# The first layer's w_in in four tiles of four slices, folded with 512 moving columns

## The chip, the cores and the metric

One core of a Trainium2 chip runs the kernel. The metric is the device time of one execution in microseconds (us), the median over several runs. Engines are called as the profile calls them: PE (TensorE matmul), PEld (its weight load), DVE (VectorE), ACT (ScalarE), POOL (GpSimd), SP (SyncE, which issues nearly all DMAs).

## The reference

An attention between tokens and a small state, then two layers of the form "matmul, nonlinearity, matmul" on the 2304 rows that it returns. Shapes: B=4, H=8, S=512 tokens and Ns=32 states per batch, D=64; model width 512, hidden width 2048. All is float32; the weights arrive as float64.

```python
scores = scale * np.matmul(x, state.transpose(0, 1, 3, 2))
a = np.exp(scores - scores.max(-1, keepdims=True))
a /= a.sum(-1, keepdims=True) + 1e-09
xread = np.matmul(a, state)                      # 512 rows per batch
...                                              # sread: the same with x and state exchanged, 32 rows per batch
x = rows of concatenate([xread, sread], axis=2)  # (2304, 512)
h = x @ w_in;  g = np.where(h > 0, h, np.exp(np.minimum(h, 0)) - 1);            x = g @ w_out
h = x @ w_in2; g = h * np.tanh(np.log1p(np.exp(np.minimum(h, 20)))); out = g @ w_out2
```

## The kernel before

**Folding.** For the tokens of batch b, xread is a product of the softmax `a` with the state, so `xread @ w_in` equals `a @ (state @ w_in)`. The kernel makes the small product m = state @ w_in once per batch (`fold`, the matmul at L523) and multiplies the softmax by it (L755, or L769 to L771), so the full w_in of the first layer is used only by the folds and by the 128 rows of the states (L745). A fold multiplies one head's 32 states by 64 rows of w_in: eight matmuls, two on the array's rows by four on its columns, lie side by side in the array, each with its own weights of 64 x 32. One call `fold(b, j0, j1)` makes m for the slices j0 to j1 of w_in (a slice is 128 of the 2048 hidden columns): it takes two PSUM banks, issues eight matmuls per step of at most two slices (so 256 moving columns), and then copies both banks to `m` (L532). A float32 matmul has two records in the trace: where the program's order says x2, the trace says x4.

**Tiles.** w_in of the first layer lies in eight tiles `w1[j // 2]` of two slices each, under the tag "w_in" of 16 buffers of 4 KB per partition. The 16 products m (four per batch, four slices each) and the 16 slices of the second layer's w_in use the same tag.

**Staging of weights.** `weight` loads a slice of float64 (L430 for the first w_in, two DMAs of 256 KB; L436 for w_out), ACT makes `wy` of its high words (L446), DVE adds the low bits and the sign (L455, L457, L468 into the w1 tile, L474 or L478 for w_out). The second layer's weights go through DRAM and come back by `reload` and `split_weight`.

**Steps.** A step is one slice j of one batch: `mm1` (h = softmax x m), `hidden` (ACT exp L788, ACT L791, DVE L795 or L798) and, two steps later, `mm2` (four accumulations acc, one per 128 tokens). The first eight steps (batch 0, slices 0 to 7) run in whole float32: h by L755, and acc by L837 for the first six of them. Later steps split each operand in two float32r parts, three matmuls each (L769 to L771, L849 to L851). Then come batch 1 with slices 0 to 7, batches 0 and 1 with slices 8 to 15, batches 2 and 3, and the second layer. Before batch b can run, `token_reads(b, hf)` makes its softmax: it loads x (`xb`, L556, two DMAs of 256 KB for each of two halves hf), transposes it on PE (`xT`, L600: two groups of four transposes, one for each DMA), makes scores (L638), the softmax on DVE and ACT, and transposes that (`pT`, L663).

**What sets the order.** No order is written by hand. `Plan.run` simulates the engines with the costs given to `add` and places next, engine by engine, the operation that can start first (ties go to the earlier due time). An operation can start when its predecessors have ended and its buffers are free; the DMA queues have a rate, `RATE` = 330 bytes per ns, and a latency of 2 us in that simulation. The result is a fixed instruction order on each engine, and an engine waits at an instruction whose semaphore has not come, whatever stands behind it. A fold's cost is given as

```python
step = min(2, j1 - j0)
...
for j in range(j0, j1, step):
    A("PE", 0.1 + mm(4 * step * P), lambda j=j: f(j), w=[(pt, j) for pt in pts], place=[m, *pts],
      lag=FOLD_AHEAD if (b, j0) == (STATES_AFTER[0], STATES_AFTER[1] + 1) else FOLD_LAG,
      r=[("sd", b, 0), ("sd", b, 1)] + [(w1[i // 2], i % 2) for i in range(j, j + step)])
```

Batch 0 makes its first eight slices by `FIRST_FOLDS` in five calls of 1, 1, 2, 2 and 2 slices, as the weights arrive; every other m is one call of four slices, in two steps of two.

Of the kernel before, what the change touches and what calls it, by code (L numbers as in the profile page):

```python
# [40 lines left out]
class Buf:  # L41
# [6 lines left out]

    def __getitem__(self, i):
        return self.t[i]  # L50


class Op:
# [162 lines left out]
def attention_elu_mish(  # L216
# [190 lines left out]
    w1, w_sb, w_back = {}, {}, {}  # L407

    def place_w1(j, k):
        return w1[j // 2].t.rearrange("p (k f) -> p k f", k=NK)[:, k, j % 2 * P:(j % 2 + 1) * P]  # L410

    loads = itertools.count()

    def weight(kind, layer, j, due=None):
        i = next(loads)
        soon = i < EARLY
        due = -20.0 + i if i < RAW_FIRST else due
        name = f"{kind}{layer}_{j}_"
# [25 lines left out]


        add("ACT", 0.68, lambda: nc.scalar.activation(y.t, words()[0].bitcast(F32), AF.Copy, scale=2.0 ** -112),  # L446
            r=[raw], w=[y])
        signs = layer == 1 and Z_FROM <= j < Z_TO
        if signs:

            add("ACT", 0.68, lambda: nc.scalar.activation(v.t, y.t, AF.Identity, bias=negative, scale=2.0 ** -60),
                r=[y, "negative"], w=[v])
        else:

            add("DVE", 0.43, lambda: nc.vector.tensor_scalar(u32(v), u32(y), 3, None, ALU.logical_shift_left),  # L455
                r=[y], w=[v])
        add("DVE", 0.69, lambda: nc.vector.scalar_tensor_tensor(  # L457
            u32(v), words()[1], 29, u32(v), ALU.logical_shift_right, ALU.bitwise_or), r=[raw, v], w=[v])
        last = (3, ALU.logical_shift_left) if signs else (0x80000000, ALU.bitwise_and)
        if kind == "in" and layer == 1:  # L460
            if j // 2 not in w1:
                w1[j // 2] = buf("w", "w_in", NF, [P, NK * 2 * P], F32, f"w1_{j // 2}_")
            to = w1[j // 2]

            def sign():
                o = to.t.bitcast(U32).rearrange("p (k f) -> p k f", k=NK)[:, :, j % 2 * P:(j % 2 + 1) * P]
                a, c = (u32(i).rearrange("p (k f) -> p k f", k=NK) for i in (y, v))
                nc.vector.scalar_tensor_tensor(o, a, last[0], c, last[1], ALU.bitwise_or)  # L468

            add("DVE", 0.69, sign, r=[y, v], w=[(to, j % 2)])  # L470
            return
        if layer == 1 and j < WHOLE_OUT:
            w = w_sb["whole", layer, j] = buf("w", f"w_{kind}", NF, [P, DM], F32, f"whole{j}_")
            add("DVE", 0.69, lambda: nc.vector.scalar_tensor_tensor(  # L474
                u32(w), u32(y), last[0], u32(v), last[1], ALU.bitwise_or), r=[y, v], w=[w])
            after_step.setdefault(index[1, 0, j], []).append(j)
            return
        add("DVE", 0.69, lambda: nc.vector.scalar_tensor_tensor(  # L478
            u32(v), u32(y), last[0], u32(v), last[1], ALU.bitwise_or), r=[y, v], w=[v])
        if layer == 2:  # L480
            add(SP, 256.0, lambda: nc.sync.dma_start(out=w2d[:, kind == "out", j, :], in_=v.t),
                r=[v], w=[("w2d", kind, j)])
            return
        split_weight(kind, layer, j, v)

    after_step = {}

    def split_weight(kind, layer, j, v):
        w = w_sb[kind, layer, j] = buf("w", f"w_{kind}", NF, [P, 2, DM], F32R, f"w_{kind}{layer}_{j}_")
        add(EITHER, {"ACT": 0.61, "DVE": 0.43}, lambda e: copy(e, w[:, 0, :], v.t), r=[v], w=[(w, 0)])  # L490
        lo, cost = (nc.gpsimd, {"POOL": 1.3}) if (kind, layer, j) in POOL_LO else (nc.vector, {"DVE": 0.69})
        add(next(iter(cost)), cost, lambda: lo.tensor_tensor(
            w[:, 1, :], v.t, w[:, 0, :].bitcast(F32), ALU.subtract), r=[v, (w, 0)], w=[(w, 1)])

    def reload(kind, j):
        v = buf("work", "wraw", 3, [P, DM], F32, f"back_{kind}_{j}_")
# [6 lines left out]

    def m_tile(b, c):
        if (b, c) not in m_sb:
            m_sb[b, c] = buf("w", "w_in", NF, [P, 2, DM], F32, f"m{b}_{c}_")
        return m_sb[b, c]

    def fold(b, j0, j1):
# [2 lines left out]
        m = m_tile(b, j0 // NC)  # L512
        pts = [bank("fold") for e in range(2)]
        n = (j1 - j0) * P
        step = min(2, j1 - j0)

        def f(j):
            w = w1[j // 2].t.rearrange("p (k f) -> p k f", k=NK)
            c = slice(j % 2 * P, (j % 2 + step) * P)
            for k in range(NK):  # L520
                for e in range(2):
                    r, l = slice(e * D, (e + 1) * D), slice(k * NS, (k + 1) * NS)
                    nc.tensor.matmul(pts[e][l, (j - j0) * P:(j - j0 + step) * P], lhsT=sd[b][r, e, k, e, :],  # L523
                                     rhs=w[r, k, c], start=True, stop=True, tile_position=(e * D, k * NS))

        for j in range(j0, j1, step):
            A("PE", 0.1 + mm(4 * step * P), lambda j=j: f(j), w=[(pt, j) for pt in pts], place=[m, *pts],
              lag=FOLD_AHEAD if (b, j0) == (STATES_AFTER[0], STATES_AFTER[1] + 1) else FOLD_LAG,
              r=[("sd", b, 0), ("sd", b, 1)] + [(w1[i // 2], i % 2) for i in range(j, j + step)])
        cols = slice(j0 % NC * P, j0 % NC * P + n)  # L530
        for e in range(2):
            A(EITHER, both(n), lambda g, e=e: copy(g, m[:, e, cols], pts[e][:, :n]),  # L532
# [203 lines left out]
    def mm1(s):  # L736
# [4 lines left out]
        if kind == 0:  # L741
            for i in range(NC):
                def f(i=i):
# [3 lines left out]

                sl = j * NC + i
                A("PE", 4 * mm(4 * P), f, w=[h], due=due,
                  r=[(w1[sl // 2], sl % 2)] + [("sread", b) for b in range(B)])  # L750
        elif kind == 1 and (blk, j) in WHOLE:
            for k in range(2):
                def f(k=k):
# [5 lines left out]
        else:  # L759
            nk = 2 if kind == 1 else NK  # L760
            for k in range(nk):
# [12 lines left out]
                    r = [(m_hl[s], 0), (m_hl[s], 1), (x1hl(blk), k)]  # L774
                else:
                    w = w_sb["in", 2, j]
                    r = [(w, 0), (w, 1), (x2[blk][0], k), (x2[blk][1], k)]
                add("PE", 3 * mm(n), f, r=r, w=[h], due=due)
        return h

# [282 lines left out]
```

## Time and profile before

| | us |
|---|---|
| device time, median of 3 runs (lowest, highest) | 753.88 (753.29, 753.99) |
| span of the profiled execution | 751.1 |
| PE busy in 0 to 20 of the span | 11.91 |
| PE busy in 20 to 45 | 23.30 |
| PE busy in 45 to 60 | 14.65 |
| PE busy in 60 to 80 | 20.00 |
| PE busy in 80 to 100 | 18.57 |
| PE busy in 100 to 742 | 641.69 |
| DVE busy in 20 to 45, and in 60 to 80 | 23.18, 18.70 |

Between 100 and 742 us PE is busy without a break, so there only its own work counts; what it waits for is found in the first 100 us. A timeline row gives the start, the length, the engine, the line, the tiles (out<-in), the shape, the count, and in brackets the idle time ahead of it with what ended it. A matmul's length contains the pipeline behind it; the time that it takes from its neighbours is the distance from its start to the next start.

### The profile page before, as it was taken

To read this page: it belongs to the slowest core of one execution; us is meant where nothing else is said; L and a number is where in the kernel's file an instruction comes from. 1 tells how busy PE (TensorE), PEld (TensorE's weight loads), DVE (VectorE), ACT (ScalarE), POOL (GpSimd) and SP (SyncE) were. 2 spreads that over 40 slices of the span, in tenths; PEclk is the share of its full clock that TensorE was granted. 3 is DMA by queue.
4 is the path that set the end of the run, shared out by engine and by line. 5 is a ranking of instruction groups with operands and counts; after the bars stand their busy time and mean duration, and the time that the engine had idled before them with its cause. 6 is when DMAs were issued, how large, how long until landed. Compare 5 with 4: busy or idle time off the path is not lost.

```text
span 751.1 us, 11051 instructions
## 1 busy us (share of the span) xinstructions
PE 732.6 (98%) x4098; PEld 598.0 (80%) x4098; DVE 556.8 (74%) x1048; ACT 425.0 (57%) x759; POOL 10.6 (1%) x27
## 2 busy tenths in 40 slices
PE   5899999999999999999999999999999999999996
PEld 5346677788777879878888888888889999999995
DVE  6988899988689895798999856565567565756564
ACT  3674767655567663577657445454455455545443
POOL 1000000010000000000000000000000000000000
PEclk8899999999999999999999999999999999999999
DMA  9953667453585543665845103000030020001001
GB/s 227 291 154 101 166 161 215 117 169 113 147 256 175 189 140 104 189 196 185 283 162 193 42 1 99 0 1 1 0 99 1 1 83 2 1 1 42 1 1 42
DMA packets 67292, 81.71 MB, mean 109 GB/s; under 512 B 22696, under 2 KB 45992, under 8 KB 67240
## 3 DMA queue, kind: packets, MB, share of 16 engines
q1 hardware_dynamic: 65028, 80.36, 36.1%
q10 hardware_dynamic: 2212, 0.66, 0.4%
q8 instruction: 32, 0.52, 0.3%
q14 instruction: 20, 0.16, 0.1%
HBM read 59.51 MB, written 21.50 MB: 108 GB/s over the span
## 4 chain that ended last, share of the span: by engine, by line
PE 94%; DMA 2%; DVE 1%; ACT 1%; issue 0%; SPq 0%; ACTq 0%
PE acc_acc L849 16%; PE acc_acc L851 15%; PE acc_acc L850 15%; PE h L769 12%; PE h L771 12%; PE h L770 12%; PE fold L523 2%; PE acc_acc L837 2%; PE h L745 2%; PE h L755 2%; DMA raw_in<-in_moe_w_in 2%; PE scores L638 1%; PE pT L663 1%; PE sr L697 1%; DMA xb<-in_x 1%; PE xT L600 1%
## 5 line engine op out<-in xcount | busy, mean ns | idle before, releaser
L788 ACT ACTIVATE e<-h 128x512 f32<-128x512 f32 (+1 forms) x148 | 83.2, 562 | 118.2 <-PE h L771 106.5
L813 ACT CAST g<-e 128x512 fp32r<-128x512 f32 (+1 forms) x142 | 82.4, 581 | 61.9 <-PE acc_acc L851 25.6
L771 PE MATMUL h<-x,w_in 128*128 128x384 f32 (+1 forms) x320 | 114.6, 358 | 0.0
L769 PE MATMUL h<-x,w_in 128*128 128x384 f32 (+1 forms) x320 | 114.4, 358 | 0.0
L770 PE MATMUL h<-x,w_in 128*128 128x384 f32 (+1 forms) x320 | 114.3, 357 | 0.0
L814 DVE TENSOR_TENSOR g<-e,g 128x512 fp32r<-128x512 f32 (+1 forms) x142 | 91.1, 642 | 22.5 <-ACT g L813 21.7
L851 PE MATMUL acc_acc<-w_out,g 128*128 128x512 f32 x272 | 106.9, 393 | 0.0
L850 PE MATMUL acc_acc<-w_out,g 128*128 128x512 f32 x272 | 106.7, 392 | 0.0
L849 PE MATMUL acc_acc<-w_out,g 128*128 128x512 f32 x272 | 105.9, 389 | 0.4 <-ACT g L813 0.4
L849 PE MATMUL acc_acc<-g,w_out 128*128 128x512 f32 x232 | 93.3, 402 | 0.0
L810 DVE TENSOR_TENSOR u<-u,e 128x384 f32<-128x384 f32 (+1 forms) x80 | 48.9, 611 | 57.7 <-ACT e L809 57.6
L850 PE MATMUL acc_acc<-g,w_out 128*128 128x512 f32 x232 | 90.5, 390 | 0.0
L851 PE MATMUL acc_acc<-g,w_out 128*128 128x512 f32 x232 | 90.5, 390 | 0.0
L808 ACT ACTIVATE e<-u,two 128x384 f32<-128x384 f32 (+1 forms) x80 | 52.8, 660 | 50.1 <-DVE u L806 49.9
L805 DVE TENSOR_SCALAR e<-e 128x384 f32<-128x384 f32 (+1 forms) x80 | 30.9, 387 | 48.2 <-ACT e L788 48.1
L769 PEld LDWEIGHTS h<-x,w_in 128*128 128x128 f32 x320 | 60.1, 188 | 7.1
L770 PEld LDWEIGHTS h<-x,w_in 128*128 128x128 f32 x320 | 60.1, 188 | 7.1
L771 PEld LDWEIGHTS h<-x,w_in 128*128 128x128 f32 x320 | 60.1, 188 | 5.0
L851 PEld LDWEIGHTS acc_acc<-w_out,g 128*128 128x128 f32 x272 | 51.0, 187 | 11.0 <-DVE g L814 0.3
L849 PEld LDWEIGHTS acc_acc<-w_out,g 128*128 128x128 f32 x272 | 51.1, 188 | 10.1 <-ACT g L813 0.9
L850 PEld LDWEIGHTS acc_acc<-w_out,g 128*128 128x128 f32 x272 | 51.0, 188 | 9.5
L849 PEld LDWEIGHTS acc_acc<-g,w_out 128*128 128x128 f32 x232 | 43.5, 188 | 13.5 <-issue 3.3
(126 smaller groups left out, 1169.7 us busy)
## 6 DMA issues: line engine op xcount, KB each, us to landing
raw_out<-in_moe_w_out SPq DMA_DIRECT2D x32, 512.0 KB, 4.3
raw_in<-in_moe_w_in SPq DMA_DIRECT2D x32, 256.0 KB, 7.3
raw_in<-in_moe_w_in SPq DMA_DIRECT2D x16, 512.0 KB, 4.2
w2d<-wv SPq DMA_DIRECT2D x32, 256.0 KB, 3.4
xb<-in_x SPq DMA_DIRECT2D x16, 256.0 KB, 4.2
x2d<-o SPq DMA_DIRECT2D x16, 256.0 KB, 2.6
xb<-in_x SPq DMA_DIRECT2D x32, 128.0 KB, 3.9
back_in<-w2d SPq DMA_DIRECT2D x16, 256.0 KB, 3.0
```

Source lines behind the costliest of these rows:

```text
L769: nc.tensor.matmul(h[:, :n], lhsT=wh, rhs=xh, start=(k == 0), stop=False)
L770: nc.tensor.matmul(h[:, :n], lhsT=wh, rhs=xl, start=False, stop=False)
L771: nc.tensor.matmul(h[:, :n], lhsT=wl, rhs=xh, start=False, stop=(k == nk - 1))
L788: add("ACT", act(n), lambda: nc.scalar.activation(E(), Hh(), AF.Exp), r=[h], w=[e])
L805: add("DVE", 0.1 + 0.00065 * n, lambda: nc.vector.tensor_scalar(E(), E(), E20, None, ALU.min), r=[e], w=[e])
L808: add("ACT", act(n) + 0.12, lambda: nc.scalar.activation(E(), U(), AF.Ln, bias=two), r=[u, "two"], w=[e])
L810: add("DVE", dve(n), lambda: nc.vector.tensor_tensor(U(), U(), E(), ALU.mult), r=[u, e], w=[u])
L813: add("ACT", act(n) + 0.01, lambda: nc.scalar.copy(g[:, 0, :n], E()), r=[e], w=[(g, 0)])
L814: add("DVE", dve(n), lambda: nc.vector.tensor_tensor(g[:, 1, :n], E(), g[:, 0, :n].bitcast(F32), ALU.subtract), r=[e, (g, 0)], w=[(g, 1)])
L849: nc.tensor.matmul(acc.t, lhsT=st[:, 0, :], rhs=mv[:, 0, :], start=fst, stop=False)
L850: nc.tensor.matmul(acc.t, lhsT=st[:, 0, :], rhs=mv[:, 1, :], start=False, stop=False)
L851: nc.tensor.matmul(acc.t, lhsT=st[:, 1, :], rhs=mv[:, 0, :], start=False, stop=lst)
```

## The change

The eight w1 tiles become four of four slices each (8 KB per partition), under a new tag "w_wide" of four buffers; the tag "w_in" shrinks from 16 to 8 buffers. A fold takes all its slices in one step: 512 moving columns where it makes four slices, one group of eight matmuls where there were two of 256 columns. Batch 0's first five calls keep their 1, 1, 2, 2 and 2 slices. In the second layer, slices 4 to 11 of w_in lie two to a tile in the "w_wide" buffers (`Half`), and the other eight in "w_in". The lines below L48 of the changed kernel stand 14 to 22 lines lower than before.

```diff
+class Half:
+    def __init__(self, base, i):
+        self.base, self.i = base, i
+    def __getitem__(self, i):
+        return self.base.t[:, self.i][i]
+
+def part(w, i):
+    return (w.base, w.i, i) if isinstance(w, Half) else (w, i)
...
-        return w1[j // 2].t.rearrange("p (k f) -> p k f", k=NK)[:, k, j % 2 * P:(j % 2 + 1) * P]
+        return w1[j // NC][:, k, j % NC * P:(j % NC + 1) * P]
...
-                w1[j // 2] = buf("w", "w_in", NF, [P, NK * 2 * P], F32, f"w1_{j // 2}_")
+                w1[j // NC] = buf("w", "w_wide", NF // NC, [P, NK, NC * P], F32, f"w1_{j // NC}_")
...
+        if kind == "in" and NC <= j < NF - NC:
+            if j % 2 == 0:
+                pairs[j // 2] = buf("w", "w_wide", NF // NC, [P, 2, 2, DM], F32R, f"w_pair{j // 2}_")
+            w = Half(pairs[j // 2], j % 2)
+        elif kind == "in":
+            w = buf("w", "w_in", NF // 2, [P, 2, DM], F32R, f"w_{kind}{layer}_{j}_")
...
-            m_sb[b, c] = buf("w", "w_in", NF, [P, 2, DM], F32, f"m{b}_{c}_")
+            m_sb[b, c] = buf("w", "w_in", NF // 2, [P, 2, DM], F32, f"m{b}_{c}_")
...
-        step = min(2, j1 - j0)
+        step = j1 - j0
...
-            c = slice(j % 2 * P, (j % 2 + step) * P)
+            c = slice(j % NC * P, (j % NC + step) * P)
...
-              r=[("sd", b, 0), ("sd", b, 1)] + [(w1[i // 2], i % 2) for i in range(j, j + step)])
+              r=[("sd", b, 0), ("sd", b, 1)] + [(w1[i // NC], i % NC) for i in range(j, j + step)])
```

The planner then places other work. PE before, early in the program, from the first h of batch 0 on (`sd_79` is the state of batch 0 and `sd_80` that of batch 1; `fold_298` makes slice 1 of batch 0, `fold_319` slices 0 to 3 of batch 1, `fold_377` slices 2 and 3 of batch 0; h_178, h_184 are the steps 0 and 1):

```order
L755 MATMUL h_178_284<-x_0_6_268,m_0_145_244 128x512 x2
...
L523 MATMUL fold_298<-w_0_28_209,sd_79 32x128
...
L523 MATMUL fold_319<-w_0_28_209,sd_80 32x256
...
L755 MATMUL h_184_331<-x_0_6_268,m_0_145_244 128x512 x2
...
L523 MATMUL fold_319<-w_1_43_316,sd_80 32x256
...
L837 MATMUL acc_0_acc_190_360<-gw_336,whole_32_355 128x512
L837 MATMUL acc_0_acc_191_365<-gw_336,whole_32_355 128x512
L523 MATMUL fold_377<-w_1_43_316,sd_79 32x256
...
L837 MATMUL acc_0_acc_192_388<-gw_336,whole_32_355 128x512
L837 MATMUL acc_0_acc_193_396<-gw_336,whole_32_355 128x512
L755 MATMUL h_187_401<-x_0_6_268,m_0_145_244 128x512 x2
```

The same place now (h_174, h_180 and h_183 are the steps 0, 1 and 2):

```order
L777 MATMUL h_174_284<-x_0_6_268,m_0_141_244 128x512 x2
...
L545 MATMUL fold_298<-w_0_28_209,sd_79 32x128
...
L777 MATMUL h_180_319<-x_0_6_268,m_0_141_244 128x512 x2
L545 MATMUL fold_329<-w_0_28_209,sd_79 32x256
...
L622 MATMUL xT_347<-ident,xb_276 128x128 x4
L622 MATMUL xT_355<-ident,xb_276 128x128 x4
L777 MATMUL h_183_361<-x_0_6_268,m_0_141_244 128x512 x2
L859 MATMUL acc_0_acc_186_377<-gw_325,whole_32_353 128x512
L859 MATMUL acc_0_acc_187_386<-gw_325,whole_32_353 128x512
L859 MATMUL acc_0_acc_188_390<-gw_325,whole_32_353 128x512
L859 MATMUL acc_0_acc_189_396<-gw_325,whole_32_353 128x512
```

Batch 1's fold has left this place (it now stands in one piece among the accumulations of step 4), the transposes of batch 1's first half of x, which stood behind step 3's accumulations before, have come here, and step 0's four accumulations now follow step 2's h.

SP's queue before, where those x are loaded (`xb_276` is the first half of batch 1, in two DMAs):

```order
L430 DMA raw_in_6_70_255<-in_moe_w_in 64x4x128 x2
L436 DMA raw_out_3_51_264<-in_moe_w_out 128x512
L556 DMA xb_276<-in_x 128x2x256 x2
L556 DMA xb_294<-in_x 128x2x256 x2
L654 DMA s2d<-raw_195 128x512
```

and now:

```order
L444 DMA raw_in_6_69_255<-in_moe_w_in 64x4x128 x2
L450 DMA raw_out_3_50_264<-in_moe_w_out 128x512
L578 DMA xb_276<-in_x 128x2x256 x2
L578 DMA xb_294<-in_x 128x2x256 x2
L676 DMA s2d<-raw_195 128x512
```

Nothing has moved here: up to this place the queue holds the same transfers in the same order.

PE where batch 1 follows on batch 0, before (`fold_746` makes slices 4 to 7 of batch 1; h_225, h_229 and h_237 are the steps 8, 9 and 10):

```order
L523 MATMUL fold_746<-w_2_58_367,sd_80 32x256
...
L769 MATMUL h_225_681<-x_1_158_649,ms_536 128x512
...
L769 MATMUL h_229_708<-x_1_158_649,ms_610 128x512
...
L523 MATMUL fold_746<-w_3_73_452,sd_80 32x256
...
L769 MATMUL h_237_795<-x_1_158_649,ms_770 128x512
```

and now:

```order
L545 MATMUL fold_737<-w_1_57_382,sd_80 32x512
...
L791 MATMUL h_221_670<-x_1_154_639,ms_619 128x512
...
L791 MATMUL h_225_699<-x_1_154_639,ms_621 128x512
...
L791 MATMUL h_233_775<-x_1_154_639,ms_764 128x512
...
L791 MATMUL h_248_790<-x_1_154_639,ms_766 128x512
```

The two pieces of this fold have become one, ahead of steps 8 and 9, and nothing stands between step 9's h and step 10's.

## Rows read from the trace of the kernel before

**Rows 1.** Page, part 1: busy us (share of the span) xinstructions.
```profile
PE 732.6 (98%) x4098; PEld 598.0 (80%) x4098; DVE 556.8 (74%) x1048; ACT 425.0 (57%) x759; POOL 10.6 (1%) x27
```

**Rows 2.** Timeline of PE, 22 to 35 us: start, length, engine, line, operation.
```profile
25.40 0.45 PE L523 MATMUL fold<-w,sd 64*32 64x128 f32 x16
26.41 0.74 PE L523 MATMUL fold<-w,sd 64*32 64x256 f32 x16 [0.56 <-ACT m L275]
27.07 1.98 PE L755 MATMUL h<-x,m 128*128 128x512 f32 x4
28.99 0.66 PE L523 MATMUL fold<-w,sd 64*32 64x256 f32 x16
...
34.43 1.02 PE L755 MATMUL h<-x,m 128*128 128x512 f32 x2
```

**Rows 3.** Timeline of all engines, 25.6 to 26.5 us.
```profile
25.64 1.29 DVE L468 SCALAR_TENSOR_TENSOR w<-wy,wv 128x512 uint32<-128x512 uint32 x2
...
26.00 0.43 ACT L275 COPY m<-fold 128x128 f32<-128x128 f32 x2
```

**Rows 4.** DMA issues, 22.3 to 22.6, then 24.8 to 25.1 us; last, us to landing.
```profile
xb<-in_x SPq DMA_DIRECT2D x1, 256.0 KB, 11.0
...
xb<-in_x SPq DMA_DIRECT2D x1, 256.0 KB, 9.9
```

**Rows 5.** Timeline of PE, 53 to 60 us.
```profile
53.18 1.04 PE L600 MATMUL xT<-ident,xb 128*128 128x128 f32 x8
54.05 1.02 PE L755 MATMUL h<-x,m 128*128 128x512 f32 x2
54.91 1.89 PE L638 MATMUL scores<-sd,xT 128*128 128x64 f32 x16
...
59.32 0.66 PE L600 MATMUL xT<-ident,xb 128*128 128x128 f32 x4 [0.35 <-ACT xT L275]
```

**Rows 6.** Timeline of PE, 100.3 to 102.5 us, around a fold in one piece.
```profile
100.44 0.39 PE L851 MATMUL acc_acc<-g,w_out 128*128 128x512 f32 x1
100.76 1.09 PE L523 MATMUL fold<-w,sd 64*32 64x256 f32 x32
101.78 0.50 PE L849 MATMUL acc_acc<-g,w_out 128*128 128x512 f32 x1
102.12 0.40 PE L850 MATMUL acc_acc<-g,w_out 128*128 128x512 f32 x1
102.35 0.39 PE L851 MATMUL acc_acc<-g,w_out 128*128 128x512 f32 x1
```

**Rows 7.** Timeline of PE, 76.8 to 82.5 us.
```profile
77.18 0.66 PE L523 MATMUL fold<-w,sd 64*32 64x256 f32 x16
77.78 0.50 PE L769 MATMUL h<-x,ms 128*128 128x512 f32 x1
...
79.36 0.66 PE L523 MATMUL fold<-w,sd 64*32 64x256 f32 x16
81.45 0.50 PE L769 MATMUL h<-x,ms 128*128 128x512 f32 x1 [1.43 <-DVE e L798]
```

**Rows 8.** Timeline of PE, 137 to 139 us.
```profile
137.56 0.66 PE L523 MATMUL fold<-w,sd 64*32 64x256 f32 x16
138.16 0.50 PE L849 MATMUL acc_acc<-g,w_out 128*128 128x512 f32 x1
```

**Rows 9.** Windows: stretch, us, busy us of each engine, PEclk, DMA share, GB/s.
```profile
7.00:13.80 6.80, 5.33 (x44) 4.57 (x42) 4.84 (x9) 3.15 (x7) 0.13 (x1) 1.00 1.14 230
13.80:24.00 10.20, 6.54 (x39) 4.66 (x38) 8.82 (x18) 4.90 (x11) 0.00 (x0) 0.50 1.12 239
24.00:40.00 16.00, 15.45 (x108) 5.83 (x107) 14.45 (x27) 11.35 (x22) 0.00 (x0) 1.00 0.98 284
```

**Rows 10.** Timeline of PE, 4 to 24 us.
```profile
4.10 2.40 PE L351 MATMUL warm<-ident 128*128 128x128 f32 x10 [4.10 <-DVE ident L335]
...
11.40 4.85 PE L638 MATMUL scores<-sd,xT 128*128 128x64 f32 x32 [1.04 <-DVE sd L275]
...
21.14 2.18 PE L663 MATMUL pT<-ident,prob 128*128 128x128 f32 x8 [1.55 <-DVE sm L656]
```

More of the change, by code (lines that the diff above doesn't have):

```diff
@@ L460, in weight @@
         if kind == "in" and layer == 1:
-            if j // 2 not in w1:
-                w1[j // 2] = buf("w", "w_in", NF, [P, NK * 2 * P], F32, f"w1_{j // 2}_")
-            to = w1[j // 2]
+            if j // NC not in w1:
+                w1[j // NC] = buf("w", "w_wide", NF // NC, [P, NK, NC * P], F32, f"w1_{j // NC}_")
+            to = w1[j // NC]
             def sign():
-                o = to.t.bitcast(U32).rearrange("p (k f) -> p k f", k=NK)[:, :, j % 2 * P:(j % 2 + 1) * P]
+                o = to.t.bitcast(U32)[:, :, j % NC * P:(j % NC + 1) * P]
                 a, c = (u32(i).rearrange("p (k f) -> p k f", k=NK) for i in (y, v))
                 nc.vector.scalar_tensor_tensor(o, a, last[0], c, last[1], ALU.bitwise_or)
-            add("DVE", 0.69, sign, r=[y, v], w=[(to, j % 2)])
+            add("DVE", 0.69, sign, r=[y, v], w=[(to, j % NC)])
             return
         if layer == 1 and j < WHOLE_OUT:
-            w = w_sb["whole", layer, j] = buf("w", f"w_{kind}", NF, [P, DM], F32, f"whole{j}_")
+            w = w_sb["whole", layer, j] = buf("w", "w_out", NF, [P, DM], F32, f"whole{j}_")
             add("DVE", 0.69, lambda: nc.vector.scalar_tensor_tensor(
@@ L484, in weight @@
         split_weight(kind, layer, j, v)
-    after_step = {}
+    after_step, pairs = {}, {}
     def split_weight(kind, layer, j, v):
-        w = w_sb[kind, layer, j] = buf("w", f"w_{kind}", NF, [P, 2, DM], F32R, f"w_{kind}{layer}_{j}_")
-        add(EITHER, {"ACT": 0.61, "DVE": 0.43}, lambda e: copy(e, w[:, 0, :], v.t), r=[v], w=[(w, 0)])
+        if kind == "in" and NC <= j < NF - NC:
[4 more added lines that the diff above has]
+            w = buf("w", "w_in", NF // 2, [P, 2, DM], F32R, f"w_{kind}{layer}_{j}_")
+        else:
+            w = buf("w", f"w_{kind}", NF, [P, 2, DM], F32R, f"w_{kind}{layer}_{j}_")
+        w_sb[kind, layer, j] = w
+        add(EITHER, {"ACT": 0.61, "DVE": 0.43}, lambda e: copy(e, w[:, 0, :], v.t), r=[v], w=[part(w, 0)])
         lo, cost = (nc.gpsimd, {"POOL": 1.3}) if (kind, layer, j) in POOL_LO else (nc.vector, {"DVE": 0.69})
         add(next(iter(cost)), cost, lambda: lo.tensor_tensor(
-            w[:, 1, :], v.t, w[:, 0, :].bitcast(F32), ALU.subtract), r=[v, (w, 0)], w=[(w, 1)])
+            w[:, 1, :], v.t, w[:, 0, :].bitcast(F32), ALU.subtract), r=[v, part(w, 0)], w=[part(w, 1)])
     def reload(kind, j):
@@ L514, in fold @@
         n = (j1 - j0) * P
-        step = min(2, j1 - j0)
+        step = j1 - j0
         def f(j):
-            w = w1[j // 2].t.rearrange("p (k f) -> p k f", k=NK)
-            c = slice(j % 2 * P, (j % 2 + step) * P)
+            w = w1[j // NC].t
+            c = slice(j % NC * P, (j % NC + step) * P)
             for k in range(NK):
@@ L749, in mm1 @@
                 A("PE", 4 * mm(4 * P), f, w=[h], due=due,
-                  r=[(w1[sl // 2], sl % 2)] + [("sread", b) for b in range(B)])
+                  r=[(w1[sl // NC], sl % NC)] + [("sread", b) for b in range(B)])
         elif kind == 1 and (blk, j) in WHOLE:
@@ L776, in mm1 @@
                     w = w_sb["in", 2, j]
-                    r = [(w, 0), (w, 1), (x2[blk][0], k), (x2[blk][1], k)]
+                    r = [part(w, 0), part(w, 1), (x2[blk][0], k), (x2[blk][1], k)]
                 add("PE", 3 * mm(n), f, r=r, w=[h], due=due)
```

## The prediction

> **What bounds the kernel now.** I read the page's busy times first: PE is busy 98% of the span [rows 1], and by the table above without a break from 100 to 742 us. So a change counts by what PE has to do, or by what it is made to wait for; DVE and ACT matter only where they release PE. Then I read the timeline of PE over the first 100 us, where its waits are, and put it beside the new instruction order. The reader is to see two things there. From 25 to 35 us PE alternates folds, h and accumulations with one short wait of 0.56 us [rows 2]. And DMA is loaded to the brim: 0.98 to 1.14 of the engines from 7 to 40 us [rows 9], so that a transfer issued at 22.3 us lands 11.0 us later, one issued at 24.8 us 9.9 us later [rows 4].
>
> **The fold itself.** One m of four slices in one go (32 records of 256 columns) holds PE from 100.76 to 101.78, that is 1.02 us; around it two matmuls start 0.32 and 0.34 us after their neighbours instead of 0.23, so the whole price is 1.02 + 0.09 + 0.11 = 1.22 us [rows 6]. Half of it alone (16 records) takes 0.60 us, with the same edges 0.80 us [rows 7, 8]. So 16 more records of 256 columns add 0.42 us, as much as one record of 512 columns in a full matmul (54.05 to 54.91 holds two, 0.43 each [rows 5]); and 16 records of 128 columns have a length of 0.45 us against 0.66 [rows 2]. The fold goes by columns, not by records. Eight matmuls of 512 columns stream as many columns as two times eight of 256: I take 1.22 us, no gain. The bounds are 0.80 us, if the number of records decided, and 1.29 us, if the new form cost its whole length of 1.09 us. A gain comes only where the two halves stood apart: 2 x 0.80 - 1.22 = 0.38 us. That is so for three of the fourteen four-slice folds: batch 1's first and second (below), and the one whose first half stands at 137.56 us and its second some us further on [rows 8]. The last gives **-0.38 us**.
>
> **Batch 1's first fold leaves the start.** Before, it lies at 26.41 and at 28.99 us, around step 1's h [rows 2]. Without it, step 1's h can start when ACT has copied slice 1 of m, at 26.00 + 0.43 = 26.43 us [rows 3], say 26.46. It holds PE for 28.99 - 27.07 = 1.92 us [rows 2], to 28.38. Then comes batch 0's fold of slices 2 and 3; its weights are ready, since DVE ends both writes at 25.64 + 1.29 = 26.93 us [rows 3]; 0.60 us, to 28.98.
>
> **What stands next is the loss.** PE's next instruction is the transpose of batch 1's first x, and PE waits there for the first DMA of `xb_276`. SP's queue is the same as before up to there, and DMA was full, so I take the landing of before: 22.3 + 11.0 = 33.3 us [rows 4]. PE idles from 28.98 to 33.3, **4.3 us**. Behind the waiting transposes stand step 2's h and step 0's accumulations, all of whose inputs are there. ACT waits with PE: the copies of these transposes are ahead of the next weights in its order, and DVE needs those. Four transposes are half of 54.05 - 53.18 = 0.87 us [rows 5], to 33.8; the second DMA lands between 33.3 and the 24.8 + 9.9 = 34.7 us of the third [rows 4], I take the middle, 34.0; with four more transposes and an edge step 2's h starts at about 34.5 us. Before, it starts at 34.43 [rows 2]. The two kernels are level in time there, but not in work. The new one still owes step 0's four accumulations, 8 records of 0.43 us = 3.43 us, and batch 1's fold, 1.22 us; it is ahead by eight transposes, 0.87 us. Sum: 0.07 + 3.43 + 1.22 - 0.87 = **+3.85 us**.
>
> **Where batch 1 follows on batch 0.** Before, PE goes from the first half fold at 77.18 over two h, the other half and a wait of 1.43 us to step 10's h at 81.45: 4.27 us. That wait is for DVE to free step 8's PSUM bank, and it runs from step 8's h: 81.45 - 77.78 = 3.67 us [rows 7]. So the second half fold was hidden in it. In one piece ahead of step 8 the fold costs its 1.02 us in front of the same chain: 1.02 + 3.67 = 4.69 us, +0.42. If the chain gets shorter, because the copy of m is then done early, up to the full saving of -0.38 is possible. I take **0.0**, the middle.
>
> **The rest at nothing.** The tiles of the second layer move no bytes and add no instruction; slices 4 to 11 wait for the last use of the first w_in, as the buffers under the old tag did, and PE has no wait from 100 to 742 us; if that cover were gone, one wait like the 1.43 us [rows 7] is what I would add. Without the clock the sum is 3.85 + 0.0 - 0.38 = **+3.5 us**.
>
> **The clock.** The granted clock was 1.00 from 7.0 to 13.8 us, 0.50 (1.2 GHz instead of 2.4) from 13.8 to 24.0, and 1.00 after [rows 9]. It fell after a hole of 1.04 us ahead of 11.40 and scores of 64 columns, and it rose 2.9 us after PE took up the pT at 21.14 us [rows 10]. At the start, too, it rose 2.9 us after the first work, the transposes at 4.10 us [rows 9, 10]. A hole of 4.3 us should make it fall again, and 2.9 us of work at half speed lose 1.45 us, of which little hides in the wait for the second DMA: I take **+1.4 us**, with bounds of 0 and of 2.3, below. That gives +4.9 us. The sum is made on the profiled execution, whose span of 751.1 us has 2.8 us around it up to the median; the change is within the span, so it goes onto the median: 753.9 + 4.9 = **758.8 us**.
>
> The Trainium skill, in "TensorE: Matmul & The Clock Gate", "Part 4: PE-mode transpose", says that transposes do not count as PE work for the full clock as other matmuls do. By that rule the clock would come back only some time after step 2's h, the late case below. The trace speaks against it: ahead of 7.0 us PE had done nothing but transposes.
>
> **Rivals.** (1) *The clock holds.* Then +3.5: 757.4 us. For it: from 24.0 us on PE has run dense work, unlike ahead of the first fall. (2) *The clock comes back late*, only 2.9 us after step 2's h at 34.5 us: the eight transposes cost their 0.87 us twice and h and accumulations lose 1.45: +2.3 instead of +1.4, 759.7 us. For it, the half-rate stretch of 10.2 us [rows 9] is the longest seen. (3) *The hole is given back.* PE's later waits of 0.35 and 1.43 us [rows 5, 7] end by ACT and DVE; if these keep working in the hole, both vanish: 758.8 - 1.8 = 757.0 us, or 755.6 with a clock that holds. Against it: ACT and DVE stand behind the same transposes, and DVE is busy 18.70 of 20 us from 60 to 80. (4) *The data is there*, on the side of not slower: if xb landed by 28.98 us, step 2's h would start at 28.98 + 0.87 + 0.1 = 29.95 instead of 34.5 and the clock would hold: 3.5 - 4.55 = -1.05, 752.8 us. It decides at 29.8 us: a landing ahead of that makes the kernel no slower. It needs 7.5 us instead of 11.0 [rows 4] with the same queue ahead of it. (5) *Records decide.* If the half price of 0.80 held for all fourteen folds, eleven would save 0.42 more, 4.6 us: 758.8 - 4.6 = 754.2 us. The 128-column row speaks against it.
>
> **How the numbers follow.** The forecast has 0.56, with 757.9 to 760.0 around it for the second landing and the 0.4 us at batch 1; (1) 0.17, (2) 0.07, (3) 0.11, (4) 0.06, (5) 0.03. The likeliest gives 758.8 us. The range reaches from 756.2 (most of (3)) to 760.4 (the late clock and the dearer batch 1). A measurement of this kernel can tell 0.2%, 1.5 us, from no change: from 752.4 to 755.4 us is the same. (4) is there, and (5), and a little of (3): same 0.10; faster 0.03 for the lowest end of (4); slower 0.87.
>
> **What would show it.** In the new profile: PE idle some 4 us ahead of the xT transposes at about 33 us, put down to the DMA of xb; step 2's h at about 34.5 to 35 us, with four accumulations right behind; PEclk below 1.00 for some us after the hole; the folds x16 of 512 columns at about 1.0 us each; from 100 us on no PE idle. A landing ahead of 30 us, a fold clearly under 0.9 us, or PE gaining on the old kernel between 35 and 85 us would make the prediction wrong.

## The result and the profile after

The changed kernel took **758.31 us** in the median (757.45 to 760.30), the kernel before 753.93 us on the same chip: a ratio of 1.0062 (95% interval 1.0047 to 1.0078; the ratios below have theirs in brackets). That is 4.4 us slower, where +4.9 us was forecast. The profiled executions' spans are 751.1 us before and 755.1 us now.

First the page of the changed kernel, part 1 (busy us, share of the span, instructions). It answers [rows 1].

```profile
PE 733.6 (97%) x3874; PEld 594.5 (79%) x3874; DVE 555.7 (74%) x1041; ACT 428.1 (57%) x766; POOL 10.5 (1%) x27
```

PE bounds this kernel too, so I went on to where it stands still. PE's timeline of the start answers [rows 2] (start us, us, engine, line, operation, then the idle time ahead and its releaser):

```profile
26.01 0.45 PE L545 MATMUL fold<-w,sd 64*32 64x128 f32 x16
26.92 1.98 PE L777 MATMUL h<-x,m 128*128 128x512 f32 x4 [0.46 <-ACT m L289]
28.84 0.66 PE L545 MATMUL fold<-w,sd 64*32 64x256 f32 x16
31.94 1.54 PE L622 MATMUL xT<-ident,xb 128*128 128x128 f32 x8 [2.44 <-DMA xb<-in_x]
33.28 3.37 PE L777 MATMUL h<-x,m 128*128 128x512 f32 x4
36.48 3.60 PE L859 MATMUL acc_acc<-gw,whole 128*128 128x512 f32 x8
```

The hole is where the forecast put it, ahead of batch 1's transposes, and it is put down to the DMA of `xb`. It is 2.44 us instead of 4.3. Behind it the same four h matmuls that took 28.84 - 26.92 = 1.92 us take 36.48 - 33.28 = 3.20 us: the clock. The granted clock by stretches (from:to, its length, busy us of each engine, PEclk, DMA share, GB/s) answers [rows 9]:

```profile
19.20:26.00 6.80, 5.51 (x12) 2.62 (x12) 6.55 (x13) 1.75 (x4) 0.00 (x0) 0.50 1.09 294
26.00:32.80 6.80, 3.85 (x43) 1.68 (x43) 4.02 (x8) 4.45 (x10) 0.00 (x0) 1.00 1.07 332
32.80:36.30 3.50, 3.50 (x8) 1.81 (x7) 2.48 (x5) 1.94 (x4) 0.00 (x0) 0.51 0.83 201
36.30:50.00 13.70, 13.70 (x47) 5.80 (x46) 11.44 (x21) 10.16 (x18) 0.00 (x0) 1.00 0.32 111
```

The clock fell to its half level (0.51: 1.2 of 2.4 GHz) for 3.4 us behind the hole, from 32.9 to 36.3 us; in the kernel before it stays at 1.00 there [rows 9]. PE stood still at no time in this stretch, so half speed cost it half of that, 1.7 us. Most of it shows on the h: ahead of the same accumulations and at full clock the four take 1.72 us (filled, below), here 3.20, which is 1.48 us more. The other 0.2 us lies on the last transposes. (The eight transposes take 33.28 - 31.94 = 1.34 us instead of 0.87 [rows 5], but the rest of that is mostly a pause between the fourth and the fifth, ahead of the fall.)

The transfer itself, by the group of tile `xb` from 15 to 60 us (issues, their first and last start; then issue to landing, min, median, max), answers [rows 4]:

```profile
L578 SPq DMA_DIRECT2D xb<-in_x x4: 367/374/384, 21.4 to 24.6; - x4
...
DMA to landing us min/median/max: 9.8/10.1/10.4
```

The first one was issued at 21.4 us and took 10.4 us; in the profile of before it was 22.3 and 11.0. The landing so came 1.5 us ahead of the forecast's 33.3 us. PE in turn got to the place 0.5 us later than forecast, at 31.94 - 2.44 = 29.50 us instead of 28.98. Both make the hole shorter.

The fold in one piece on 512 columns answers [rows 6]:

```profile
104.00 0.39 PE L873 MATMUL acc_acc<-g,w_out 128*128 128x512 f32 x1
104.32 1.09 PE L545 MATMUL fold<-w,sd 64*32 64x512 f32 x16
105.34 0.50 PE L871 MATMUL acc_acc<-g,w_out 128*128 128x512 f32 x1
105.67 0.39 PE L872 MATMUL acc_acc<-g,w_out 128*128 128x512 f32 x1
```

It holds PE for 105.34 - 104.32 = 1.02 us, with edges of 0.32 and 0.33 us. Before it was 1.02 us, with 0.32 and 0.34. Half the records, the same time. Where batch 1 follows on batch 0, these rows answer [rows 7]:

```profile
80.72 1.09 PE L545 MATMUL fold<-w,sd 64*32 64x512 f32 x16
81.74 0.50 PE L791 MATMUL h<-x,ms 128*128 128x512 f32 x1
...
85.05 0.50 PE L791 MATMUL h<-x,ms 128*128 128x512 f32 x1 [1.65 <-DVE e L820]
```

The wait is 1.65 us instead of 1.43, and the fold in one piece now lies ahead of it. And there is one wait that the kernel before does not have:

```profile
170.86 0.40 PE L793 MATMUL h<-x,ms 128*128 128x512 f32 x1
171.90 1.25 PE L622 MATMUL xT<-ident,xb 128*128 128x128 f32 x8 [0.64 <-DVE den L723]
```

To see where the time was lost I set the same accumulation of both traces side by side and took the difference of their starts, called the lag from here on. One row of each kernel shows how, the first accumulation with split operands (step 6's), of before and then of the changed kernel:

```profile
70.45 0.40 PE L849 MATMUL acc_acc<-g,w_out 128*128 128x512 f32 x1
```

```profile
74.00 0.40 PE L871 MATMUL acc_acc<-g,w_out 128*128 128x512 f32 x1
```

At 70 us the changed kernel is 3.55 us behind, at 109 us 3.57, at 189 us 4.14, and from 332 us on 4.06 us. So nearly all of it is lost ahead of 42 us, nothing at the batch transition (where batch 1 follows on batch 0), and 0.6 us around 172 us. Not all of the 3.55 us is the change's, though: 0.61 us stands already at the fold of 128 columns (26.01 against 25.40 us [rows 2]), ahead of anything that moved on PE. The start differs by that much from one execution to the next; tiles_only below, with the order of before, has this fold at 27.02 us. That left four questions: is it the 512 columns or the order; how much is the hole and how much the clock; why did the hole come out shorter; and what is the wait at 172 us.

### The profile page after: what moved, and what is told of

Its sections match the earlier page's. It is cut to its first block, busy times and chain, and to the rows that moved or that the text cites. A ratio compares the mean times of both kernels' runs of the same rounds, so it can differ in the third digit from the quotient of the medians.

```text
span 755.1 us, 10598 instructions
## 1 busy us (share of the span) xinstructions
PE 733.6 (97%) x3874; PEld 594.5 (79%) x3874; DVE 555.7 (74%) x1041; ACT 428.1 (57%) x766; POOL 10.5 (1%) x27
## 4 chain that ended last, share of the span: by engine, by line
PE 94%; DMA 4%; DVE 1%; SPq 0%; ACT 0%; issue 0%; ACTq 0%
PE acc_acc L871 15%; PE acc_acc L873 15%; PE acc_acc L872 15%; PE h L791 12%; PE h L793 12%; PE h L792 12%; PE acc_acc L859 3%; DMA raw_in<-in_moe_w_in 2%; PE fold L545 2%; PE h L767 2%; PE h L777 2%; DMA xb<-in_x 1%; PE scores L660 1%; PE xT L622 1%; PE sr L719 1%; PE acc_att L871 0%
## 5 line engine op out<-in xcount | busy, mean ns | idle before, releaser
L793 PE MATMUL h<-x,w_in 128*128 128x384 f32 (+1 forms) x160 | 57.3, 358 | 0.0
L793 PE MATMUL h<-x,w_pair 128*128 128x384 f32 (+1 forms) x160 | 57.3, 358 | 0.0
L791 PE MATMUL h<-x,w_in 128*128 128x384 f32 (+1 forms) x160 | 57.2, 358 | 0.0
L791 PE MATMUL h<-x,w_pair 128*128 128x384 f32 (+1 forms) x160 | 57.2, 358 | 0.0
L792 PE MATMUL h<-x,w_in 128*128 128x384 f32 (+1 forms) x160 | 57.1, 357 | 0.0
L792 PE MATMUL h<-x,w_pair 128*128 128x384 f32 (+1 forms) x160 | 57.1, 357 | 0.0
```

The source lines that it names most:

```text
L791: nc.tensor.matmul(h[:, :n], lhsT=wh, rhs=xh, start=(k == 0), stop=False)
L792: nc.tensor.matmul(h[:, :n], lhsT=wh, rhs=xl, start=False, stop=False)
L793: nc.tensor.matmul(h[:, :n], lhsT=wl, rhs=xh, start=False, stop=(k == nk - 1))
```

## The experiments

### Which part of the change: the columns, the tiles or the wait

**tiles_only** keeps the four wide tiles and the shared pairs of the second layer, and folds in two pairs again:

```diff
-        step = j1 - j0
+        step = min(2, j1 - j0)
```

> The changed kernel with its four wide tiles and the pairs of the second layer, but a fold still goes in steps of two slices (256 moving columns, each step waiting for its own two slices). Theory A (the loss is PE waiting at the transposes of batch 1's first x, which the planner moves ahead because a fold in one step cannot start before all its four slices are there): the planner gives the order of the kernel before, no such wait, 753.9 us within 1. Rival B (the wide tiles or the shared buffers of the second layer cost the time themselves): about 758 us. Rival C (512 moving columns cost it): 753.9, as A; the next run tells these two apart.

It measured 753.96 us, a ratio of 1.0005 (0.9996 to 1.0014). PE's order at the start is that of before again, batch 1's first fold standing in two halves around step 1's h, and there is no hole:

```profile
28.03 0.74 PE L545 MATMUL fold<-w,sd 64*32 64x256 f32 x16 [0.56 <-ACT m L289]
28.70 1.98 PE L777 MATMUL h<-x,m 128*128 128x512 f32 x4
30.61 0.66 PE L545 MATMUL fold<-w,sd 64*32 64x256 f32 x16
```

The wide tiles and the shared buffers cost nothing that can be told (the interval ends at 0.14%, 1.1 us). The 1.6 us by which these rows stand behind before's [rows 2] come from the start; they are not the tiles' price.

**whole_wait** goes the other way: the kernel before, with its own tiles and its own matmuls of 256 columns; only the first pair of a fold already waits for all four slices, as a fold in one piece must (the lists of what each step reads now name all slices of the fold):

```diff
-              r=[("sd", b, 0), ("sd", b, 1)] + [(w1[i // 2], i % 2) for i in range(j, j + step)])
+              r=[("sd", b, 0), ("sd", b, 1)] + [(w1[i // 2], i % 2) for i in range(j0, j1)])
```

> The kernel before, with its eight tiles and 256 columns, in which each step of a fold is told to wait for all the slices of the fold and nothing else is changed. PE's order at the start then is that of the changed kernel: transposes of batch 1's x ahead of step 2. Theory A: a hole of 2.4 to 4.3 us ahead of these transposes, put down to the DMA of xb, most times a stretch at half clock after it, 758.3 us (757.4 to 760.3). Rivals B and C (wide tiles, 512 columns): 753.9 us, since neither is there.

It measured 758.02 us, a ratio of 1.0059 (1.0046 to 1.0073): the whole loss, without a fold on 512 columns and without a wide tile. PE's start, and the clock:

```profile
28.99 0.66 PE L523 MATMUL fold<-w,sd 64*32 64x256 f32 x16
32.91 1.08 PE L600 MATMUL xT<-ident,xb 128*128 128x128 f32 x4 [3.26 <-DMA xb<-in_x]
34.53 1.09 PE L600 MATMUL xT<-ident,xb 128*128 128x128 f32 x4 [0.53 <-DMA xb<-in_x]
35.40 3.61 PE L755 MATMUL h<-x,m 128*128 128x512 f32 x4
```

```profile
32.00:38.75 6.75, 5.31 (x12) 2.97 (x13) 2.92 (x5) 2.26 (x4) 0.00 (x0) 0.50 1.04 307
```

So what costs is the wait for four slices: the planner can't place the fold early, takes batch 1's transposes in its stead, and their data are not there.

### The hole and the clock

**filled** is the changed kernel with three idle matmuls of 512 columns (they write a PSUM tile that nobody reads) between the fold of batch 0 and the transposes. PE works through the hole, and the hole's time stays lost (a part of the edit):

```diff
+            def burn():
+                for _ in range(HOLE):
+                    nc.tensor.matmul(full.t, lhsT=ident, rhs=w1[0].t[:, 0, :], start=True, stop=True)
```

> The changed kernel with three idle float32 matmuls of 512 columns (2.6 us) put on PE into the hole ahead of batch 1's transposes; their result is thrown away and all else stands as it was. If the half clock behind the hole is a part of the loss of its own (1.7 us in the profile of the changed kernel): granted clock 1.00 right through 26 to 50 us, and 756.6 us. If only the hole counts: 758.3 us as the changed kernel, or up to 0.5 us more where the filling ends after the x has landed.

It measured 756.87 us, a ratio of 1.0044 (1.0032 to 1.0057), as expected.

```profile
29.29 2.84 PE L626 MATMUL full<-w,ident 128*128 128x512 f32 x6
31.97 1.04 PE L634 MATMUL xT<-ident,xb 128*128 128x128 f32 x8
32.84 1.88 PE L790 MATMUL h<-x,m 128*128 128x512 f32 x4
34.56 3.60 PE L872 MATMUL acc_acc<-gw,whole 128*128 128x512 f32 x8
```

```profile
25.50:48.00 22.50, 22.04 (x102) 9.67 (x101) 18.69 (x34) 16.49 (x31) 0.00 (x0) 1.00 0.72 215
```

The transposes start no earlier than in the changed kernel (31.97 us), but the clock stays at 1.00, and the h take 34.56 - 32.84 = 1.72 us instead of 3.20. In the times 758.3 - 756.9 = 1.4 us come back by work that does nothing. That difference alone is weak, since the intervals of the two ratios overlap (1.0032 to 1.0057, and 1.0047 to 1.0078); the rows carry it. From the fold of 128 columns to 70 us filled falls 1.16 us behind before's trace, and the changed kernel 2.94 us.

**late_xt** takes the hole away without a different fold: the loads of batch 1's x stay where they are, but their transposes may not be placed before step 4.

```diff
-    token_reads(1, 0)
-    token_reads(1, 1)
+    for hf in range(2):
+        early_x[1, hf] = load_x(1, hf)
...
+    for hf in range(2):
+        begin(GATE_FIRST, token_reads, 1, hf)
...
+GATE_FIRST = 4
```

> The changed kernel, with the loads of batch 1's x where they are, but its transposes and softmax held back until step 4's h. Theory A: the wait of 2.4 us and the half clock of 3.4 us behind it are gone, 755.1 - 2.5 - 1.7 = 750.9 us of span, 753.7 us with the 2.8 around it; no PE gap over 1 us between 25 and 45 us. Rivals B and C: about 757.5 us, since tiles and columns are those of the changed kernel.

It measured 755.42 us, a ratio of 1.0025 (1.0015 to 1.0035): 2.9 us come back, 1.7 less than expected. The hole is gone; batch 1's fold now stands in its place:

```profile
28.61 0.66 PE L545 MATMUL fold<-w,sd 64*32 64x256 f32 x16
29.88 1.09 PE L545 MATMUL fold<-w,sd 64*32 64x512 f32 x16 [0.61 <-ACT m L289]
30.91 1.98 PE L779 MATMUL h<-x,m 128*128 128x512 f32 x4
```

At 70 us this kernel is 0.23 us ahead of the one before. The miss is further on, at the batch transition: the wait there has grown to 1.99 us, and behind it the clock falls:

```profile
81.60 0.50 PE L793 MATMUL h<-x,ms 128*128 128x512 f32 x1 [1.99 <-DVE e L822]
```

```profile
83.25:86.50 3.25, 3.25 (x10) 2.48 (x9) 3.19 (x7) 1.32 (x2) 0.00 (x0) 0.50 0.00 0
```

**hidden_fold** tests that reading. It is late_xt with batch 1's next fold (slices 4 to 7) held back until step 9, so that it lies inside that wait:

```diff
-                begin(max(0, index[1, b, c * NC] - GATE_M), fold, b, c * NC, (c + 1) * NC)
+                begin(LATE_FOLD if (b, c) == (1, 1) else max(0, index[1, b, c * NC] - GATE_M), fold, b, c * NC, (c + 1) * NC)
...
+LATE_FOLD = 9
```

> late_xt (the reads of batch 1's tokens held back behind step 4) with one edit more: the fold of batch 1's slices 4 to 7 is held back to step 9, so that its eight matmuls lie between step 9's h and step 10's h, in TensorE's wait at the batch transition. late_xt measured 755.42 us against 753.5 before; its wait there was 1.99 us, with the clock at half for 3.4 us behind it (1.7 us lost). If that wait is for batch 1's softmax-free path e (L820) and not for the fold, the fold's 1.0 us lies inside it: the wait falls under 1.1 us, the clock stays at full, and the time is 755.4 - 1.0 - 1.7 = 752.7 us, below the kernel before. Rival: h waits for something that the fold itself delays (its eviction), the wait only moves: 755.4 us, clock fall kept.

```profile
77.99 1.09 PE L545 MATMUL fold<-w,sd 64*32 64x512 f32 x16
79.85 0.50 PE L793 MATMUL h<-x,ms 128*128 128x512 f32 x1 [0.77 <-DVE e L822]
```

```profile
78.00:96.00 18.00, 17.23 (x88) 13.56 (x88) 16.41 (x31) 13.44 (x25) 0.77 (x2) 1.00 0.59 134
```

The fold went into the wait, the wait fell from 1.99 to 0.77 us, the clock stayed at 1.00, and the time came to 753.29 us (expected 752.7), a ratio of 0.9992 (0.9983 to 1.0001). So late_xt's miss was this wait and its clock.

**again_1** and **again_2** are the changed kernel itself, one execution each, to see why the hole was shorter than forecast.

> The changed kernel itself, profiled once more, to see how much its hole differs from one execution to the next. Its first profile had a hole of 2.44 us with batch 1's x landing at 31.8 us, at 757.45 us, the lowest of its four times (757.45 to 760.30); the same order of the start in cost_old had a hole of 4.39 us, landing at 34.5 us, at 759.82 us, the highest of its six. Theory: the hole, and the half clock behind it, are what spreads the times of the changed kernel: a time of about 758.3 us goes with a hole of about 3.3 us, 760 us with one over 4 us. Rival: the hole is near 2.4 us in each execution of the changed kernel and the spread comes from the first 25 us.

> The same kernel as again_1 once more, with the same two expectations.

They took 758.74 and 759.63 us. PE in the first and in the second:

```profile
32.88 1.84 PE L622 MATMUL xT<-ident,xb 128*128 128x128 f32 x8 [2.85 <-DMA xb<-in_x]
34.51 2.90 PE L777 MATMUL h<-x,m 128*128 128x512 f32 x4
37.24 3.60 PE L859 MATMUL acc_acc<-gw,whole 128*128 128x512 f32 x8
```

```profile
31.99 1.02 PE L622 MATMUL xT<-ident,xb 128*128 128x128 f32 x4 [2.49 <-DMA xb<-in_x]
33.81 1.08 PE L622 MATMUL xT<-ident,xb 128*128 128x128 f32 x4 [0.81 <-DMA xb<-in_x]
34.69 3.62 PE L777 MATMUL h<-x,m 128*128 128x512 f32 x4
38.10 4.00 PE L859 MATMUL acc_acc<-gw,whole 128*128 128x512 f32 x8
```

The clock of the second:

```profile
32.00:38.80 6.80, 5.99 (x13) 3.20 (x14) 2.92 (x5) 2.71 (x5) 0.00 (x0) 0.51 0.91 281
```

The hole is not one number. It was 2.44, 2.85 and 2.49 + 0.81 = 3.30 us, and the half clock behind it lasted 3.4, 3.4 and 6.8 us. With them the lag at the accumulation of above is 3.55, 4.31 and 5.58 us, and the times are 757.45, 758.74 and 759.63 us. So the direction of the theory holds in these three executions: a longer hole and a longer half clock go with a longer time. Its figures don't: a hole of 3.3 us was to give 758.3 us and came with 759.63.

The rival, the first 25 us, has its share too. What PE waits for is the landing, and a landing is the issue plus the way: the first DMA of x was issued at 21.4, 22.4 and 22.3 us and took 10.4, 10.3 and 9.5 us. In again_1 x landed later because it was issued later. In again_2 it was the second DMA that came late, and the clock that stayed low. The fold of 128 columns, PE's own start, stood at 26.01, 26.54 and 26.01 us. How much of the changed kernel's spread of 2.9 us (757.45 to 760.30; before's four times beside it lie within 1.1) goes to the start and how much to the hole and its clock, three executions can't settle.

### What comes later: the order behind it

**cost_old** undoes one number of the planner, its price for a four-slice fold, so that the order of the start (and the hole) stays and the later order changes:

```diff
-            A("PE", 0.1 + mm(4 * step * P), lambda j=j: f(j), w=[(pt, j) for pt in pts], place=[m, *pts],
+            A("PE", (0.2 + 2 * mm(2 * step * P)) if step == NC else 0.1 + mm(4 * step * P), lambda j=j: f(j), w=[(pt, j) for pt in pts], place=[m, *pts],
```

> The changed kernel with one number of the planner undone: a fold of four slices is planned at the cost of the two pairs that it replaced (0.2 + two times the time of 256 columns a matmul). The start and its hole are the same in the order; behind step 5 the order differs. Theory: the wait of 0.64 us at 171.9 us (xT waiting for DVE's den) came from the order that the planner made with the cheaper price; without it 758.3 - 0.6 = 757.7 us, with the hole of 2.4 us and the clock's fall at 33 us kept. Rival: the wait belongs to the fold in one piece itself, then it stays and the time is 758.3 us.

It measured 757.54 us (754.78 to 759.82), a ratio of 1.0046 (1.0032 to 1.006). Batch 2's transposes now come in fours, with no wait for den (the normalisation of a state read), and the lag goes from 6.74 us at 109 us to 6.45 at 189 us, where the changed kernel's goes from 3.57 to 4.14. So the wait at 172 us belongs to the order that the cheaper price made, and not to the fold. The median fits the expected 757.7, but it can't carry that, since this profiled execution had the largest hole of all:

```profile
34.59 1.94 PE L622 MATMUL xT<-ident,xb 128*128 128x128 f32 x8 [4.39 <-DMA xb<-in_x]
```

**after_hidden** is the changed kernel with hidden_fold's `LATE_FOLD = 9` alone; the early transposes and the hole stay.

> The changed kernel with one edit, the fold of batch 1's slices 4 to 7 held back to step 9 as in hidden_fold; the early xT and its hole stay. Theory: at the batch transition the fold's 1.2 us lies in TensorE's wait (1.65 us in the changed kernel), which shrinks to about 0.4 us; the time is 758.3 - 1.2 = 757.1 us. Rival: the wait grows by what the fold took from it and nothing is gained: 758.3 us.

```profile
82.53 1.09 PE L545 MATMUL fold<-w,sd 64*32 64x512 f32 x16
84.25 0.50 PE L791 MATMUL h<-x,ms 128*128 128x512 f32 x1 [0.64 <-DVE e L820]
```

In the trace it did what was expected: the lag fell from 3.97 us at 70 us to 2.76 at 91 us, by 1.21. In the time it can't be seen: 758.11 us (757.64 to 759.93), a ratio of 1.0067 (1.0053 to 1.008). The spread of over 2 us that the start and the hole make covers it, and in the profiled execution the stretch behind the last matmuls was 0.9 us longer than the changed kernel's; why is open.

**hidden_old** joins hidden_fold and cost_old, **hidden_den** is hidden_fold with the state read's normalisation planned 0.5 us earlier:

```diff
-        A("DVE", 0.5, norm, r=[pt], w=[den, (st, hf)], lag=1.0)
+        A("DVE", 0.5, norm, r=[pt], w=[den, (st, hf)], lag=0.5)
```

> Both edits together: hidden_fold with the four-slice fold planned at its old price. If the two act apart, it is hidden_fold less the wait of 0.64 us at 170 us: 752.1 us. If the old price moves the start or the transition again, it lies at or above hidden_fold.

> hidden_fold with one number of the planner more: the normalisation of a state read (den) is planned half a microsecond earlier. Up to 150 us the order of every engine is that of hidden_fold; behind it batch 2's transposes (xT) are cut into the four transposes of one DMA at a time and come later, as they did in the kernel before. Theory: hidden_fold's wait of 0.64 us at 167 us goes, and nothing else changes: 753.3 - 0.6 = 752.7 us, 0.15% below the kernel before. Rival: as in hidden_old, taking this wait away brings another or costs as much in edges: 753.3 us or above.

Both take the wait for den away. hidden_old gained nothing: 753.97 us, ratio 1.0006 (0.9997 to 1.0014), 1.9 us above what was expected. Its new order brought a pT forward, which waits and pushes PE 0.38 us back against hidden_fold:

```profile
73.67 0.63 PE L687 MATMUL pT<-ident,prob 128*128 128x128 f32 x4 [0.20 <-DVE prob L682]
```

That is not all. Around den it gains 0.94 us, and at 300 us it stands 0.56 us ahead of hidden_fold. Then one fold holds PE for 321.94 - 319.88 = 2.06 us, where a fold of four slices takes 1.02 in the rows above:

```profile
319.88 2.13 PE L545 MATMUL fold<-w,sd 64*32 64x512 f32 x16
321.94 0.50 PE L873 MATMUL acc_acc<-g,w_out 128*128 128x512 f32 x1
```

These 1.04 us put it 0.47 us behind. Why this fold took twice its time, and whether it does so in each execution, is open; the last but one fold, which this is, took 1.36 us in again_1 and 1.02 in the changed kernel's first profile.

hidden_den came to 752.84 us (expected 752.7), a ratio of 0.9993 (0.9984 to 1.0002), the lowest of all; it still can't be told from the kernel before.

**rate215** tells the planner that the loads are slower; the edit is this one number:

```diff
-BACKLOG, RATE = 3.0, 330.0
+BACKLOG, RATE = 3.0, 215.0
```

> The changed kernel with the planner's DMA rate put at 215 in place of 330 bytes per ns, and nothing else. The planner then knows that batch 1's x lands late, and its order holds batch 1's xT back behind the folds of slices 0, 1 and 2 to 3 and of step 2 by itself, as the order of before did by the wait for two pairs. Theory (the loss is an early xT, put there because the planner takes the loads for faster than they are): the hole at 32 us and the clock's fall go, and with the pair merged the time is 753.9 us (as tiles_only), 754.5 with the wait of 0.64 us kept. Rival: the rate changes other loads' order too and brings waits of its own: 756 us or more.

It measured 755.85 us, a ratio of 1.0021 (1.0006 to 1.0037): close to the rival. The hole is gone, as the theory has it (batch 1's fold starts at 32.46 us after 0.61 us for ACT's copy of m). But the new rate orders the very start anew as well: the first fold waits 2.66 us for a weight, and the half clock of the start lasts until 30.8 us (24.1 in before's trace, 26.0 in the changed kernel's). The loads of batch 1's x have moved too, from 21.4 to 36.1 us. So the early transposes do hang on the planner's picture of the loads, but this run changes too much at once to test their place alone; as a cure it is too blunt.

## Why the prediction was right, step by step

- **The fold by its columns, no gain: right.** 1.02 us in 16 records against 1.02 us in 32, with the same edges. Rival 5 (records decide) is out.
- **Batch 1's first fold leaves the start, the transposes move up: right.** whole_wait shows that this alone is the loss. The forecast had step 1's h 1.06 us after the start of the fold of 128 columns; it is 0.91.
- **The hole: right in place and cause, too large in size.** The size came out wrong since this step took one landing, before's 33.3 us, for the landing, and set it against PE's own start in that one trace. The first x landed at 31.9, 32.9 and 32.0 us, in the last case with the second DMA at 33.8, and PE got there at 29.5, 30.0 and 29.5 us, not at 28.98. Step 2's h, forecast for 34.5 us, started at 33.28, 34.51 and 34.69 us. The forecast's own middle for the second DMA, 34.0 us, mattered in one of the three.
- **The clock: right in its price, +1.4 forecast, 1.7 us by the rows; the count behind it does not hold.** The forecast had the clock fall in the hole and come back 2.9 us after the first transposes. It fell at 32.9 us, 0.9 us after PE had taken up work, and came back at 36.3 us. From the first transpose behind the hole to full clock it was 4.3, 3.7 and 6.9 us in the three executions, from step 2's h 3.0, 2.0 and 4.2 us. The start was no better a measure: there full clock came 2.9 us after the first transposes in the one trace that the forecast had (7.0 us), and about 4.9, 5.1 and 4.1 us after them in these three (9.0, 9.2 and 8.2 us; the starts of neighbouring transposes are 0.21 us apart ahead of it and 0.11 behind it). So 2.9 us, read twice in one trace, is no constant, and that the 1.4 us which came of it lie near the 1.7 is in part luck.
- **Rival 2 (the clock comes back late, 759.7 us)** is what again_2 did with its clock, 6.8 us at half and 759.63 us: not another case, but the upper end of the same one. The number fits better than its parts, since rival 2 had a hole of 4.3 us.
- **Whether transposes count for the clock** is not settled by what follows the hole. At the start all four traces (before, and the three executions) come to full clock with nothing but transposes behind them, as the prediction said of before. The Trainium skill, in "TensorE: Matmul & The Clock Gate", "Part 4: PE-mode transpose", says that transposes do not count as PE work for the full clock as other matmuls do. These four starts speak against it.
- **Hole, order and clock together** were +5.25 us (3.85 + 1.4) at this place; the three executions show a lag of 3.55, 4.31 and 5.58 us. Of that 0.61, 1.14 and 0.61 us stand already at the fold of 128 columns, so from that fold to 70 us the three lost 2.94, 3.17 and 4.97 us, 3.7 in the mean.
- **Rival 3 (the hole is given back)** is there in a small part: before's wait of 0.35 us for ACT [rows 5] has gone in the changed kernel. The other, of 1.43 us, has grown to 1.65.
- **The batch transition, 0.0: right**, but as the middle between two bounds and not by a working. The lag is 3.55 us ahead of it and 3.56 behind. The fold does stand with its 1.02 us in front of the chain, and the chain from step 8's h to step 10's took 85.05 - 81.74 = 3.31 us instead of 3.67; why it got shorter is open. That the fold could be hidden in the wait is shown by after_hidden's 1.21 us.
- **The last pair, -0.38:** cost_old, which has no wait beside it, shows -0.29 from 109 to 189 us, hidden_den -0.28. In the changed kernel -0.29 and the wait of 0.64 would make 3.57 to 3.92; it is 4.14. So the place of this wait costs 0.2 to 0.3 us more than the wait itself, and where that lies I could not find.
- **"From 100 us on no PE idle": wrong.** The wait at 172 us was not foreseen. The instruction order showed batch 2's eight transposes in one row, right behind a state read, and I didn't look for what they wait for. It adds 0.6 us and more.
- So 758.8 against 758.3 is in part luck, from misses of opposite sign: the hole with its order and clock was too large by some 1.5 us (5.25 against a mean of 3.7), a wait of 0.6 us was missing, and the executions of the changed kernel started 0.6 to 1.1 us behind the one trace that the sum was set on.

## What to carry to other kernels

An edit that merges two operations merges their waits too: ask first which of the two inputs comes last, what the planner or the order puts into the place that becomes free, and whether the data of that are there. A hole of two or three microseconds on PE is dearer than it looks when the clock falls behind it (here by another 1.7 us in the first profile), so it pays to put work of any use into it; a fold that was due anyway took 1.2 us off the wait and kept the clock up. And a landing that is read from one execution is one draw: when a term of the sum is "it waits for this DMA", take the spread of the start for it and not a single number. The same holds for a lag between two traces: see first how far apart they stand ahead of the change.

## What was not expected of the hardware

- The half clock behind a hole lasted 3.4 us behind waits of 1.99 us (late_xt), 2.15 us (after_hidden), 2.44 and 2.85 us (the changed kernel), and 6.8 us behind 3.26 + 0.53 us (whole_wait), 2.49 + 0.81 us (again_2) and 4.39 us (cost_old). Behind waits of 1.43 us (before), 1.65 us (the changed kernel at 85 us) and 0.77 us (hidden_fold) it stayed at 1.00.
- Behind the shorter holes the fall came late: in the changed kernel 0.9 us after PE was at work again (work from 31.94, half from 32.9 us), in late_xt 1.5 us after it (81.60 and 83.1 us). The matmuls that pay are those behind the hole.
- The same transfer, with the same queue ahead of it, landed at 31.3 us in one execution (filled) and at 34.5 us in another (cost_old): it was issued between 21.4 and 23.3 us and took 9.5 to 11.2 us. The DMA engines were busy all along (1.09 and 1.07 of their time in the changed kernel's stretches above).
